# A transformer block on one core: the last 256 columns of the attention gate move from TensorE's rows to GpSimd

## The chip, the cores and the metric

The kernel runs on one core of a Trainium2 chip, written engine by engine: TensorE (PE in the profile) multiplies matrices, VectorE (DVE), ScalarE (ACT) and GpSimd (POOL) work on tiles in SBUF, the on-chip memory of 128 partitions, and SyncE (SP) issues most DMA transfers. TensorE writes to PSUM, which has eight banks. Each engine works through its own list of instructions in order and waits on semaphores where it needs another's result. The metric is the device time of one execution in microseconds (us).

## The reference, cut to what matters

The kernel computes one block of a diffusion transformer: two sequences (batch 2) of 256 tokens, width D = 1152, two attention heads, an MLP of width 4608, all in bfloat16. Six vectors per sequence, computed from a conditioning vector c, shift, scale and gate the two halves of the block.

```python
mod = (_silu(c) @ w_mod).reshape(B, 6, 1, D)
shift_a, scale_a, gate_a, shift_m, scale_m, gate_m = [mod[:, i] for i in range(6)]
h = _layernorm(x, axis=-1) * (1 + scale_a) + shift_a
qkv = (h @ wqkv).reshape(B, N, 3, H, Dh)
...
a = ...softmax(q k^T * Dh ** (-0.5)) v ... @ wo
x = x + gate_a * a
h2 = _layernorm(x, axis=-1) * (1 + scale_m) + shift_m
m = _gelu(h2 @ w_fc1) @ w_fc2
return x + gate_m * m
```

The change is about `gate_a`: 2 x 1152 numbers, each a product of a 1152-vector (the SiLU of c) with a column of `w_mod`.

## The kernel before, in words

All matrices are cut along the contraction into KT = 9 blocks of 128 partitions. The order of TensorE's work is written out by hand: scale and K projection first, then the shift, Q projection, attention scores S with softmax interleaved with the V projection (`v_proj`), the transposes of the softmax tiles (`pt_transposes`), the rest of V, the attention output (`pv`), the output projection (`wo_tile`), the second layer norm, FC1 with GELU and FC2. TensorE and SyncE keep the order in which the program names their work. VectorE, ScalarE and GpSimd get theirs from a planner in the program (`Sched.schedule`): each operation carries an estimated cost, and the planner places an operation when, by these estimates, its inputs are ready, the longest remaining chain first. What it places stays in that order at run time: an instruction whose inputs are late holds up everything behind it on its engine.

The attention gate is made in two ways. Its first FG = 896 columns (NG = 7 groups of 128) are accumulated on VectorE in `attn_gate`. For each block kt and each sequence b, one instruction multiplies the block's weights by a number per partition, L1059 for the first block and L1062 for the others, which also adds the running sum `ACCA`. The 128 partitions are then added up: transposition of 32x32 squares (L1067), a reduction (L1069), three moves and three additions that bring the four groups of 32 partitions together (L1073, L1076), a cast (L1078) and a last transposition (L1079) to a layout in which the gate can be stored to a scratch tensor in DRAM (`st_ga`, from GpSimd's queue).

The last 256 columns come from `rows`, on TensorE: matmuls with two output rows, four of them side by side in the array, 352 columns wide for bank 3 (64 of the gate's, as a quarter of 256, and 288 of the MLP's shift and scale) and 288 wide for bank 4. ScalarE copies the gate's part out (`rows_ev`, L688), and two DMA from GpSimd's queue store it to the scratch tensor (`st_g`). VectorE transposes the rest (L1046).

SyncE's queue then reads the whole gate back, broadcast to all partitions, into `GA` (two transfers, `ld_g`). They stand in its queue behind the first two loads of FC1's weights and ahead of the next two, of the MLP gate's weights and of two quarters of FC2's. In `wo_tile`, VectorE multiplies each 128x384 tile of the output projection by the gate (L1161), which frees one of four PSUM banks for TensorE, GpSimd adds the residual (L1162), and layer norm statistics follow (L741 to L745, L1166), then the normalisation on ScalarE (L1167) and TensorE's transposes of the result (`xn2_T`).

The weights of all these columns lie in one tile, `WMODR`. It is loaded in two sets of three transfers: the columns that VectorE accumulates (`ld_ga`), then, behind the V projection's weights (`ld_wv`), all others (`ld_modr`).

VectorE also does the softmax's maxima (L1001), the normalisation (L1009) and half of the copies out of PSUM (L690). These share its list with the gate's accumulation.

Of the kernel before, what the change touches and what calls it, by code (L numbers as in the profile page):

```python
# [492 lines left out]
F32 = mybir.dt.float32  # L493
ALU = mybir.AluOpType
# [5 lines left out]
D = 1152  # L500
# [8 lines left out]
F0 = 9  # L509
KC = 5  # L510
KG = 6
NG = 7
FG = NG * 128


# [4 lines left out]
def c_act(n, aps=0):  # L520
    return 190.0 + 0.8 * n + 75.0 * aps


def c_dve_psum32(n):
    return 110.0 + 1.13 * n


def c_dve_psum16(n):
    return 110.0 + 0.57 * n
# [14 lines left out]
def build_kernel(nc, x, c, wqkv, wo, w_mod, w_fc1, w_fc2, out):  # L544
    S = Sched()
# [3 lines left out]
    scratch = scratch_t.ap()  # L549
    with (  # L550
# [4 lines left out]
        def sb(off, nbytes, dt=BF16):  # L555
            assert off % 4 == 0 and off + nbytes <= ARENA_BYTES, (off, nbytes)
            v = arena[:, off // 2:(off + nbytes) // 2]
            if dt == F32:
                v = v.bitcast(F32)
            return v  # L560

        def ps32(bank, c0=0, n=512):
            return psum[:, bank * 512 + c0: bank * 512 + c0 + n]
# [7 lines left out]
        W1 = 20736  # L571
        O_A, O_B, O_C, O_R = 0, W1, 2 * W1, 3 * W1
# [7 lines left out]
        O_GA = O_PT + 4096  # L580
        mo = [O_GA + 4608]

        def misc(nbytes):
            o = mo[0]
            mo[0] += (nbytes + 3) // 4 * 4
            assert mo[0] <= ARENA_BYTES
            return o

        def wmat(o, f):
            return sb(o, KT * f * 2).rearrange("p (k f) -> p k f", k=KT)  # L590
# [7 lines left out]
        WMODR = wmat(O_R + W1, 3 * D)  # L598
# [18 lines left out]
        GA = [sb(O_GA + b * 2304, 2304) for b in range(2)]  # L617
        GM = [sb(o + 18432, 2304) for o in (O_A, O_C)]
        XN2 = [sb(O_R + 4 * W1 - (i + 1) * 2304, 2304) for i in range(4)]
        ROWS = sb(O_R + 4 * W1 - 5 * 2304, 2304)[:, 0:288 - 32 * NG]  # L620
        ACCA = sb(O_R, FG * 8, F32).rearrange("p (b d) -> p b d", b=2)
        ACTA = sb(O_R + FG * 8, FG * 8, F32).rearrange("p (b d) -> p b d", b=2)
        GPA = sb(O_R + FG * 16, FG, F32).rearrange("p (q b g) -> p q b g", q=4, b=2)
        GBA = sb(O_R + FG * 17, 128)[0:32, :]
        GTA = sb(O_R + FG * 17 + 128, 128)[0:32, :]
        T1 = [sb(O_X + i * 1536, 1536, F32) for i in range(3)]
        OST = [sb(O_X + 4608 + i * 768, 768) for i in range(3)]
        gt_offs = ([O_P + i * 1024 for i in range(8)] + [O_B + i * 1024 for i in range(20)]
# [11 lines left out]
        ST32 = sb(misc(72), 72, F32)  # L640
# [4 lines left out]
        MT = sb(misc(2304), 2304, F32)  # L645
# [26 lines left out]
        def dma(dst, src, nbytes, name, is_out=False, eng="sp", run=4096):  # L672
            eff = 1.0 if run >= 4096 else (1.08 if run >= 2304 else (1.15 if run >= 1536 else (1.3 if run >= 1024 else 1.42)))
            return S.op(eng, 500.0 if eng == "sp" else 150.0, lambda e: e.dma_start(dst, src), reads=[src], writes=[dst],  # L674
                        name=name, dma_bytes=nbytes * eff, is_out=is_out)

        def dve(cost, fn, reads, writes, name):
            return S.op("dve", cost, fn, reads=reads, writes=writes, name=name)

        def act(cost, fn, reads, writes, name):  # L680
            return S.op("act", cost, fn, reads=reads, writes=writes, name=name)

        def pool(cost, fn, reads, writes, name):
            return S.op("pool", cost, fn, reads=reads, writes=writes, name=name)

        def copy_on(eng, dst, src, n, psum16, name):
            if eng == "act":
                act(c_act(n), lambda e: e.activation(out=dst, in_=src, func=ACTF.Copy), [src], [dst], name)  # L688
            else:
                dve(c_dve_psum16(n) if psum16 else c_dve_psum32(n), lambda e: e.tensor_copy(dst, src), [src], [dst], name)  # L690
# [12 lines left out]
        for (ka, kb, cuts) in ((0, KC, (0, 2, 5, 8, 9)), (KC, KT, (0, 3, 6, 9))):  # L703
            w = (kb - ka) * P
# [10 lines left out]
        def wfc1_load(q):  # L715
# [5 lines left out]
             reads=[ONES], writes=[IDENT], name="ident")  # L721
# [34 lines left out]
        for t in range(4):  # L756
# [13 lines left out]
            for part, c0, c1 in ((("a", 0, KC * P), ("b", KC * P, D)) if t == 3 else (("", 0, D),)):  # L770
                xi, xo = X[:, t, c0:c1], XN[:, t, c0:c1]
                dve(c_dve_fast(c1 - c0), lambda e, xi=xi, xo=xo, m=m, rs=rs: e.tensor_scalar(out=xo, in0=xi, scalar1=m, scalar2=rs,
                                                                                           op0=ALU.subtract, op1=ALU.mult),
# [37 lines left out]
        def quad_mm(bank, w, g0, g1, kt, fresh=True):  # L811
            n = 32 * (g1 - g0)
            for q in range(4):
                o = psum[32 * q:32 * q + 2, bank * 512:bank * 512 + n].rearrange("p (g c) -> p g c", c=32)
                mm(o, ST[:, kt:18:9], quads(w, g0, g1, q), kt == 0 and fresh, kt == KT - 1, tile_position=(0, 32 * q),
                   skip_group_check=not fresh)
# [136 lines left out]
        for kt in range(KT):  # L953
            for b in range(2):
                src, dst = HK[:, kt, b * 256:(b + 1) * 256], HX[:, kt, b * 256:(b + 1) * 256]
# [74 lines left out]
            copy_on("act", V[:, t, ci * CH:(ci + 1) * CH], o, CH, False, "v_ev%d_%d" % (t, ci))  # L1030


        row_parts = ((3, NG, 18), (4, 18, 27))

        last_red = [None]

        def rows():
            S.unit("pe", KT * (864 - 32 * NG) / 2.4 + 500.0, "rows")
            for kt in range(KT):
                for bank, g0, g1 in row_parts:  # L1040
                    quad_mm(bank, WMODR[:, kt, :], g0, g1, kt)
            n = 288 - 32 * NG
            copy_on("act", ROWS, ps32(3, 0, n), n, False, "rows_ev")
            for i, (bank, c0) in enumerate(((3, n), (4, 0))):
                src, dst = ps32(bank, c0, 288), MT[:, i * 288:(i + 1) * 288]
                u = dve(c_dve_psum32(288), lambda e, src=src, dst=dst: e.transpose(dst, src), [src], [dst], "mt_%d" % i)  # L1046
                S.order_after(u, last_red[0])
            sc, so = MT[:, 288:576].rearrange("p (k r) -> p k r", r=32)[:, :, 0:2], SC1M.rearrange("p (k b) -> p k b", b=2)
            dve(170, lambda e: e.tensor_scalar(out=so, in0=sc, scalar1=1.0, scalar2=None, op0=ALU.add), [sc], [so], "sc1m")
            for b in range(2):  # L1050
                dma(scratch[0, b, FG:D].rearrange("(k q c) -> q k c", q=4, c=32), ROWS[b:128:32, :].rearrange("p (k c) -> p k c", c=32),
                    2304 - 2 * FG, "st_g%d" % b, eng="pool")

        def attn_gate():
            for kt in range(KT):
                for b in range(2):
                    o, w, s1 = ACCA[:, b, :], WMODR[:, kt, 0:FG], ST32[:, b * 9 + kt:b * 9 + kt + 1]
                    if kt == 0:
                        dve(150 + FG * 0.6, lambda e, o=o, w=w, s1=s1: e.tensor_scalar(out=o, in0=w, scalar1=s1, scalar2=None, op0=ALU.mult),  # L1059
                            [w, s1], [o], "ga_%d_%d" % (b, kt))  # L1060
                    else:
                        dve(150 + FG * 1.1, lambda e, o=o, w=w, s1=s1: e.scalar_tensor_tensor(out=o, in0=w, scalar=s1, in1=o, op0=ALU.mult, op1=ALU.add),  # L1062
                            [w, s1, o], [o], "ga_%d_%d" % (b, kt))
            pool(100, lambda e: e.memset(GBA, 0.0), [], [GBA], "gba0")
            for b in range(2):
                a_, t_ = ACCA[:, b, :], ACTA[:, b, :]
                dve(150 + FG * 1.1, lambda e, a_=a_, t_=t_: e.transpose(t_, a_), [a_], [t_], "ga_T%d" % b)  # L1067
                t3, o = t_.rearrange("p (g r) -> p g r", r=32), GPA[:, 0, b, :]
                last_red[0] = dve(150 + FG * 1.1, lambda e, t3=t3, o=o: e.tensor_reduce(out=o, in_=t3, axis=AX.X, op=ALU.add), [t3], [o], "ga_red%d" % b)  # L1069
            gp = GPA.rearrange("p q b g -> p q (b g)")  # L1070
            for q in range(1, 4):
                i_, o_ = gp[32 * q:32 * q + 32, 0, :], gp[0:32, q, :]
                dve(200, lambda e, i_=i_, o_=o_: e.tensor_copy(o_, i_), [i_], [o_], "ga_mv%d" % q)  # L1073
            for a_, b_ in ((0, 1), (2, 3), (0, 2)):
                x_, y_ = gp[0:32, a_, :], gp[0:32, b_, :]
                dve(200, lambda e, x_=x_, y_=y_: e.tensor_tensor(out=x_, in0=x_, in1=y_, op=ALU.add), [x_, y_], [x_], "ga_add%d" % b_)  # L1076
            g0, gb = GPA[0:32, 0, :, :], GBA.rearrange("p (b g) -> p b g", b=2)[:, :, 0:4 * NG]
            dve(200, lambda e: e.tensor_copy(gb, g0), [g0], [gb], "ga_bf")  # L1078
            dve(200, lambda e: e.transpose(GTA, GBA), [GBA], [GTA], "ga_t")  # L1079
            for b in range(2):  # L1080
                dma(scratch[0, b, 0:FG].rearrange("(g c) -> g c", c=32), GTA[0:4 * NG, 32 * b:32 * b + 32], FG * 2, "st_ga%d" % b, eng="pool")

        def mlp_gate(prev):
            for b in range(2):
# [59 lines left out]
        def acc_bank():  # L1144
            b = acc[acc_rr[0] % len(acc)]
            acc_rr[0] += 1
            return b
# [76 lines left out]
        pt_transposes(1, 1)  # L1224
        v_proj(2, 0)
        rows()
        wfc1_load(0)
        wfc1_load(1)
# [31 lines left out]
        k = acc_rr[0] % 4  # L1260
# [12 lines left out]
        for t in range(4):  # L1273
            b = t // 2
# [3 lines left out]
            for (c0, c1) in pieces:  # L1278
                w = c1 - c0
                S.unit("pe", JT * c_mm(w), "fc2_%d_%d" % (t, c0))  # L1280
                o = ps32(acc_bank(), 0, w)
# [62 lines left out]
```

## Time and profile before

| | |
|---|---|
| median of 3 runs | 243.71 us (243.59 to 245.18) |
| the profiled execution, its own time | 243.42 us |
| its span in the profile | 241.7 us |
| TensorE busy (PE) | 235.7 us, 98% of the span |
| VectorE (DVE) / ScalarE (ACT) / GpSimd (POOL) busy | 115.9 / 68.0 / 21.4 us |
| granted TensorE clock | 1.00 |

The span runs from the first to the last instruction; the 1.7 us between it and the execution's own time lie around it. A line of the timeline gives the start and the length in us, the engine, the line of the program, the operation, what it writes and reads, shapes and count, and in brackets how long the engine had been idle and what ended that. A line of the groups gives the total busy time, the mean of one in ns, and the idle time before.

### The profile page before, as it was taken

How to read it: one execution, taken by the hardware profiler on the slowest of the kernel's cores; microseconds unless marked ns; L12 is line 12 of the kernel's file. 1: busy time of each engine (PE TensorE's matmuls, PEld its weight loads, DVE VectorE, ACT ScalarE, POOL GpSimd, SP SyncE). 2: the span in 40 equal slices, each digit the busy share in tenths (PEclk: the TensorE clock that was granted, in tenths of full speed). 3: DMA queues.
4: the chain of work that ended last, by engine and by line, in shares of the span. 5: the costliest groups of instructions: out<-in, count | busy, mean ns of one | idle time of the engine just before them, and what ended most of it. 6: DMA issues, size and time to landing. Idle time of an engine off the chain costs nothing.

```text
span 241.7 us, 3956 instructions
## 1 busy us (share of the span) xinstructions
PE 235.7 (98%) x1691; PEld 144.3 (60%) x1699; DVE 115.9 (48%) x229; ACT 68.0 (28%) x137; POOL 21.4 (9%) x38
## 2 busy tenths in 40 slices
PE   6899999999999999999999999999999999999995
PEld 2688844466657666898544444444556666566664
DVE  2654358888994589669999500000122111111112
ACT  4940540546324126973322222333000000000000
POOL 1300000000021476300000110000000000000000
DMA  6999999999994999999963499000000000000000
GB/s 220 369 374 391 390 387 386 404 414 407 391 356 124 321 379 391 392 355 394 343 209 86 122 342 376 8 0 3 0 16 19 16 16 16 19 19 27 22 17 16
DMA packets 30427, 51.58 MB, mean 213 GB/s; under 512 B 1611, under 2 KB 16971, under 8 KB 30411
## 3 DMA queue, kind: packets, MB, share of 16 engines
q1 hardware_dynamic: 29888, 50.73, 58.8%
q0 software_dynamic: 352, 0.60, 0.8%
q8 instruction: 13, 0.21, 0.4%
q10 hardware_dynamic: 171, 0.01, 0.0%
q14 instruction: 3, 0.02, 0.0%
HBM read 50.15 MB, written 1.19 MB: 212 GB/s over the span
## 4 chain that ended last, share of the span: by engine, by line
PE 94%; DMA 3%; SPq 1%; issue 0%; DVE 0%
PE psum L693 92%; DMA arena<-in_wqkv_dram 3%; PE psum L696 2%; SPq L674 1%; DVE arena L1286 0%; DVE arena L1287 0%
## 5 line engine op out<-in xcount | busy, mean ns | idle before, releaser
L693 PE MATMUL psum<-arena 128*128 128x384 bf16 (+9 forms) x1602 | 232.4, 313 | 2.8 <-POOL arena L719 1.5
L693 PEld LDWEIGHTS psum<-arena 128*128 128x128 bf16 (+2 forms) x1610 | 139.0, 97 | 92.0 <-issue 3.8
L1286 DVE TENSOR_TENSOR arena<-psum,arena 128x384 f32<-128x384 f32 (+2 forms) x13 | 6.9, 528 | 88.5 <-PE psum L693 88.5
L1196 ACT ACTIVATE arena<-psum 128x512 bf16<-128x512 f32 (+1 forms) x45 | 22.8, 511 | 42.2 <-PE psum L693 42.2
L688 ACT ACTIVATE arena<-psum 128x512 bf16<-128x512 f32 (+7 forms) x35 | 18.4, 550 | 37.5 <-PE psum L693 37.5
L1091 DVE SCALAR_TENSOR_TENSOR arena<-arena 128x1152 f32<-128x1152 bf16 x16 | 21.3, 1409 | 0.0
L1062 DVE SCALAR_TENSOR_TENSOR arena<-arena 128x896 f32<-128x896 bf16 x16 | 17.7, 1145 | 0.0
L1162 POOL TENSOR_TENSOR arena<-arena 128x384 f32<-128x384 f32 x12 | 10.9, 912 | 13.3 <-DVE arena L1161 11.1
L674 POOL DMA_DIRECT2D dit_scratch<-arena x6 | 3.6, 603 | 92.6 <-ACT arena L688 53.1
L741 DVE BATCH_NORM_STATS2 arena<-arena 128x6 f32<-128x384 f32 (+1 forms) x18 | 9.5, 550 | 4.0 <-DMA arena<-in_x_dram 3.9
L690 DVE CAST arena<-psum 128x512 bf16<-128x512 f32 x11 | 7.5, 690 | 7.4 <-PE psum L693 7.4
L1161 DVE TENSOR_TENSOR arena<-psum,arena 128x384 f32<-128x384 f32 x12 | 6.7, 555 | 3.8 <-PE psum L693 3.8
L1167 ACT ACTIVATE arena<-arena 128x1152 bf16<-128x1152 f32 x4 | 5.4, 1344 | 9.8 <-DVE arena L1166 9.8
L696 PE MATMUL psum<-arena 128*128 128x128 bf16 (+1 forms) x89 | 7.1, 219 | 0.4 <-DMA arena<-in_c_dram 0.4
L696 PEld LDWEIGHTS psum<-arena 128*128 128x128 bf16 (+1 forms) x89 | 5.8, 98 | 2.4 <-DMA arena<-in_c_dram 1.3
L1287 DVE TENSOR_TENSOR arena<-arena 128x384 bf16<-128x384 f32 (+2 forms) x13 | 6.9, 528 | 0.5
L1186 ACT ACTIVATE arena<-psum,arena 128x128 bf16<-128x128 bf16 x16 | 6.1, 455 | 3.0 <-PE psum L696 2.2
L1183 DVE TENSOR_SCALAR arena<-psum,arena 128x128 bf16<-128x128 bf16 x20 | 5.5, 336 | 2.9 <-PE psum L696 2.9
L1005 ACT ACTIVATE arena<-psum,arena 128x256 bf16<-128x256 f32 x8 | 3.7, 469 | 0.4 <-DVE arena L1002 0.3
L745 POOL TENSOR_TENSOR arena<-arena 128x1 f32<-128x1 f32 x6 | 3.3, 553 | 4.5 <-DVE arena L744 4.3
L1001 DVE TENSOR_REDUCE arena<-psum 128x2 f32<-128x512 f32 x4 | 2.7, 686 | 0.9 <-PE psum L693 0.9
L1059 DVE TENSOR_SCALAR arena<-arena 128x896 f32<-128x896 bf16 x2 | 1.3, 684 | 3.6 <-DMA arena<-in_w_mod_dram 3.6
(60 smaller groups left out, 54.1 us busy)
## 6 DMA issues: line engine op xcount, KB each, us to landing
arena<-in_w_fc_dram SPq DMA_DIRECT2D x9, 1152.0 KB, 8.1
arena<-in_w_fc_dram SPq DMA_DIRECT2D x4, 2592.0 KB, 17.5
arena<-in_w_mod_dram SPq DMA_DIRECT2D x3, 1920.0 KB, 19.7
arena<-in_wqkv_dram SPq DMA_DIRECT2D x18, 288.0 KB, 10.0
arena<-in_w_mod_dram SPq DMA_DIRECT2D x3, 864.0 KB, 12.6
arena<-in_wqkv_dram SPq DMA_DIRECT2D x1, 2592.0 KB, 16.9
arena<-in_wo_dram SPq DMA_DIRECT2D x1, 2592.0 KB, 26.1
arena<-in_w_mod_dram SPq DMA_DIRECT2D x1, 2592.0 KB, 18.2
```

Source lines behind the costliest of these rows:

```text
L688: act(c_act(n), lambda e: e.activation(out=dst, in_=src, func=ACTF.Copy), [src], [dst], name)
L690: dve(c_dve_psum16(n) if psum16 else c_dve_psum32(n), lambda e: e.tensor_copy(dst, src), [src], [dst], name)
L693: S.instr(lambda e: e.matmul(o, lhsT=l, rhs=r, start=st, stop=sp, **kw), reads=[l, r], writes=[o])
L696: S.instr(lambda e: e.transpose(o, i_, idn), reads=[i_, idn], writes=[o])
L741: dve(550, lambda e, s=s, o=o: e.bn_stats(out=o, in_=s), [s], [o], "bn_%s_%d" % (tag, ci))
L1062: dve(150 + FG * 1.1, lambda e, o=o, w=w, s1=s1: e.scalar_tensor_tensor(out=o, in0=w, scalar=s1, in1=o, op0=ALU.mult, op1=ALU.add), [w, s1 ...
L1091: u = dve(1300, lambda e, o=o, w=w, s1=s1: e.scalar_tensor_tensor(out=o, in0=w, scalar=s1, in1=o, op0=ALU.mult, op1=ALU.add), [w, s1, o], ...
L1161: dve(550, lambda e, o=o, ga=ga, x1c=x1c: e.tensor_tensor(out=x1c, in0=o, in1=ga, op=ALU.mult), [o, ga], [x1c], "wo_t1_%d_%d" % (t, ci))
L1162: S.op("pool", 930, lambda e, xs=xs, x1c=x1c: e.tensor_tensor(out=x1c, in0=x1c, in1=xs, op=ALU.add), reads=[x1c, xs], writes=[x1c], name=" ...
L1196: act(c_act(ntok), lambda e: e.activation(out=dst, in_=o, func=ACTF.Gelu_apprx_tanh), [o], [dst], "gelu_%d_%d" % (f, tok0))
L1286: dve(c_dve_psum32(w), lambda e, o=o, gm=gm, t1=t1: e.tensor_tensor(out=t1, in0=o, in1=gm, op=ALU.mult), [o, gm], [t1], "fc2_t1_%d_%d" % ( ...
L1287: dve(c_dve_32(w), lambda e, t1=t1, x1c=x1c, ost=ost: e.tensor_tensor(out=ost, in0=t1, in1=x1c, op=ALU.add), [t1, x1c], [ost], "fc2_out_%d ...
```

## The change

NG goes from 7 to 9, so that the accumulated part of the gate is all 1152 columns. `ACCA` keeps one layout; VectorE accumulates its first DG = 896 columns as before, GpSimd the last 256. GpSimd makes a block's contribution in two instructions, a multiplication into a temporary tile (`GTMP`, four buffers in the place of `GA`) and an addition into `ACCA`, since the fused form is VectorE's. VectorE's transpositions and reductions run over 1152 columns instead of 896, for each of the two sequences, and `mt`, the transposition of the rows, no longer waits for ScalarE's copy. The gate's row part, its copy and its two stores go; TensorE's row matmuls for bank 3 shrink from 352 to 288 columns. The store of the gate keeps two transfers in another cut (64 rows of 32 columns, then 8). The loads of `ld_ga` grow by 256 columns per block, those of `ld_modr` shrink by as many.

```diff
-NG = 7
+NG = 9
+DG = 7 * 128
 FG = NG * 128
...
-        row_parts = ((3, NG, 18), (4, 18, 27))
+        row_parts = ((3, 9, 18), (4, 18, 27))
...
-            n = 288 - 32 * NG
-            copy_on("act", ROWS, ps32(3, 0, n), n, False, "rows_ev")
-            for i, (bank, c0) in enumerate(((3, n), (4, 0))):
-                src, dst = ps32(bank, c0, 288), MT[:, i * 288:(i + 1) * 288]
+            for i, bank in enumerate((3, 4)):
+                src, dst = ps32(bank, 0, 288), MT[:, i * 288:(i + 1) * 288]
...
-            for b in range(2):
-                dma(scratch[0, b, FG:D].rearrange("(k q c) -> q k c", q=4, c=32), ROWS[b:128:32, :].rearrange("p (k c) -> p k c", c=32),
-                    2304 - 2 * FG, "st_g%d" % b, eng="pool")
...
                 for b in range(2):
-                    o, w, s1 = ACCA[:, b, :], WMODR[:, kt, 0:FG], ST32[:, b * 9 + kt:b * 9 + kt + 1]
...
+                    for eng, c0, c1, ns in (("dve", 0, DG, 1.1), ("pool", DG, FG, 2.3)):
+                        o, w, s1 = ACCA[:, b, c0:c1], WMODR[:, kt, c0:c1], ST32[:, b * 9 + kt:b * 9 + kt + 1]
+                        if kt == 0:
+                            S.op(eng, 150 + (c1 - c0) * ns, lambda e, o=o, w=w, s1=s1: e.tensor_scalar(out=o, in0=w, scalar1=s1, scalar2=None, op0=ALU.mult),
+                                 reads=[w, s1], writes=[o], name="ga_%s_%d_%d" % (eng, b, kt))
+                        elif eng == "pool":
+                            tmp = GTMP[:, kt % 2 * 2 + b, :]
+                            S.op(eng, 600, lambda e, o=tmp, w=w, s1=s1: e.tensor_scalar(out=o, in0=w, scalar1=s1, scalar2=None, op0=ALU.mult),
+                                 reads=[w, s1], writes=[tmp], name="ga_mul_%d_%d" % (b, kt))
+                            S.op(eng, 600, lambda e, o=o, t=tmp: e.tensor_tensor(out=o, in0=o, in1=t, op=ALU.add),
+                                 reads=[o, tmp], writes=[o], name="ga_acc_%d_%d" % (b, kt))
+                        else:
+                            S.op(eng, 150 + (c1 - c0) * ns, lambda e, o=o, w=w, s1=s1: e.scalar_tensor_tensor(out=o, in0=w, scalar=s1, in1=o, op0=ALU.mult,
+                                                                                                          op1=ALU.add),
+                                 reads=[w, s1, o], writes=[o], name="ga_%s_%d_%d" % (eng, b, kt))
...
-            for b in range(2):
-                dma(scratch[0, b, 0:FG].rearrange("(g c) -> g c", c=32), GTA[0:4 * NG, 32 * b:32 * b + 32], FG * 2, "st_ga%d" % b, eng="pool")
+            lin = scratch[0].rearrange("b (g c) -> (b g) c", c=32)
+            dma(lin[0:64].rearrange("(j p) c -> p j c", j=2), GTA[:, 0:64].rearrange("p (j c) -> p j c", j=2), 4096, "st_ga0", eng="pool")
+            dma(lin[64:72], GTA[0:8, 64:96], 512, "st_ga1", eng="pool")
```

In the changed program the lines shift: L1056 is the first multiplication (on both engines), L1060 and L1062 are GpSimd's further multiplications and its additions, L1065 is VectorE's accumulation step, L1071 and L1073 the transposition and reduction, L1077 to L1083 the moves, additions, cast and last transposition. The planner also places VectorE's work anew: the accumulation steps stand in nearly the same places among the softmax steps, while the three additions, the cast and the last transposition of the gate stand between the copies of the attention output (L691), which stood behind all of them before.

## The prediction, made before the changed kernel was run

> **What bounds the kernel now.** I read the page first (busy shares, chain that ended last), then the timeline of each engine around the gate, then the groups by form.
>
> ```profile
> span 241.7 us, 3956 instructions
> PE 235.7 (98%) x1691; PEld 144.3 (60%) x1699; DVE 115.9 (48%) x229; ACT 68.0 (28%) x137; POOL 21.4 (9%) x38
> PE 94%; DMA 3%; SPq 1%; issue 0%; DVE 0%
> ```
>
> TensorE is busy from 10.9 us to the end, and the chain runs through it: work taken from it is gained one to one, and any wait put into it is lost one to one. So two questions decide: how much shorter is TensorE's own work, and what does TensorE wait for that it found ready before? The second is read from the moments when VectorE's results are due:
>
> ```profile
> 57.86 0.39 PE L696 MATMUL psum<-arena 128*128 128x128 bf16 x4
> 59.54 0.39 PE L696 MATMUL psum<-arena 128*128 128x128 bf16 x4
> 61.23 0.39 PE L696 MATMUL psum<-arena 128*128 128x128 bf16 x4
> 62.91 0.39 PE L696 MATMUL psum<-arena 128*128 128x128 bf16 x4
> ```
>
> These are the transposes of the four softmax tiles. Each needs a normalisation on VectorE (L1009), and the timeline of VectorE shows how full that engine is before them:
>
> ```profile
> 44.91 4.33 DVE L1062 SCALAR_TENSOR_TENSOR arena<-arena 128x896 f32<-128x896 bf16 x4
> 49.15 0.69 DVE L1001 TENSOR_REDUCE arena<-psum 128x2 f32<-128x512 f32 x1
> ...
> 61.61 0.69 DVE L1009 TENSOR_TENSOR arena<-arena 128x512 bf16<-128x512 bf16 x1
> 62.21 2.21 DVE L1062 SCALAR_TENSOR_TENSOR arena<-arena 128x896 f32<-128x896 bf16 x2
> ...
> 72.08 0.23 DVE L1079 STREAM_TRANSPOSE arena<-arena 32x64 bf16<-32x64 bf16 x1
> ...
> 78.05 0.69 DVE L690 CAST arena<-psum 128x512 bf16<-128x512 f32 x1 [0.18 <-PE psum L693]
> ...
> 80.39 0.56 DVE L1161 TENSOR_TENSOR arena<-psum,arena 128x384 f32<-128x384 f32 x1 [0.77 <-PE psum L693]
> ```
>
> The last normalisation ends at 62.30 and is due at 62.91: 0.6 us of slack. From 37 to 70 us VectorE is busy 30.1 of 33 us. The gate leaves VectorE at 72.3 (L1079), is stored, read back from 75.78, and its first half lands 3.5 us later, at 79.3, just ahead of the first use at 80.39 (L1161). The kernel's slack lies in these two places, 0.6 and 1.1 us.
>
> One more reading, from the timeline of both engines, carries the forecast:
>
> ```profile
> 88.34 0.92 POOL L1162 TENSOR_TENSOR arena<-arena 128x384 f32<-128x384 f32 x1
> 88.64 0.63 DVE L1166 SCALAR_TENSOR_TENSOR arena<-arena 128x1 f32<-128x1 f32 x1
> 92.72 0.92 POOL L1162 TENSOR_TENSOR arena<-arena 128x384 f32<-128x384 f32 x1
> 93.11 0.55 DVE L1166 SCALAR_TENSOR_TENSOR arena<-arena 128x1 f32<-128x1 f32 x1
> 99.57 0.16 DVE L1166 SCALAR_TENSOR_TENSOR arena<-arena 128x1 f32<-128x1 f32 x1
> ```
>
> The same one-column instruction takes 0.16 us alone, but 0.63 and 0.55 when GpSimd is adding: it ends at 89.27 and 93.66, the GpSimd adds at 89.26 and 93.64. An instruction of VectorE with two SBUF operands is held until the running GpSimd instruction is done. BN_STATS (one SBUF operand) keeps 0.55 under the same adds. The gate's L1062 is that two-operand instruction, 16 times, and the normalisation L1009 too.
>
> **The change, part by part.** Rows on TensorE: 36 matmuls of 352 columns become 288. Four run side by side (72 matmuls of these rows take 2.5 us), and nine of 384 columns take 1.46 us, 2.36 columns per ns; 9 x 64 / 2.36 = 0.24 us less. That is all TensorE gains. ScalarE's L688 copy of the rows (0.22) and two stores on POOL's queue (1.39) go, none of them on the path.
>
> Loads: the three gate loads ahead of WV grow from 672 to 864 KB. They landed 1.9 us apart, so each takes 0.55 longer; the gate starts at 37.9 instead of 37.3, and WV lands at 49.4 instead of 47.8, due at 51.7: hidden, with 2.3 us left. The row loads behind shrink by as much.
>
> GpSimd: 18 multiplications and 16 additions of 128x256. The trace has neither shape.
>
> ```profile
> L1162 POOL TENSOR_TENSOR arena<-arena 128x384 f32<-128x384 f32 x12 | 10.9, 912 | 13.3 <-DVE arena L1161 11.1 <-DVE arena L744 2.1
> L1062 DVE SCALAR_TENSOR_TENSOR arena<-arena 128x896 f32<-128x896 bf16 x16 | 17.7, 1145 | 0.0
> ```
>
> Addition: 0.912 us for 384 columns with some 0.17 fixed (the 18-column cast of L735 takes 0.19) gives 0.66; bounds 0.50 and 0.67. Multiplication, one tensor read: from that cast (0.19) and the 128-column select of L719 (0.28), 0.0008 us a column, 0.39; bounds 0.30 and the addition's 0.67. I take 0.66 and 0.39, the nearest rows: 16 x 0.66 + 18 x 0.39 = 17.6 us, mean 0.52 (0.40 to 0.67).
>
> The hold: each two-operand instruction of VectorE should find a GpSimd instruction running, and the next GpSimd instruction then waits for it in turn (L754 took 0.83 instead of 0.57 when issued under a VectorE L772). I price one mean GpSimd instruction, 0.52, per L1062, L1009 and also the two L1059 that open the gate. Along the new VectorE order: gate from 37.9; 2 x (0.60 + 0.52) + 3 x (1.07 + 0.52) = 44.9; two copies, 46.2; four L1062, 52.6; first maximum 53.2 (before: 49.8). Then maxima (0.61), five more L1062 and four normalisations (0.60 + 0.52) alternate; these end at 58.4, 61.9, 64.2 and 68.6. Queued behind each held instruction are the softmax steps, and TensorE's transposes wait for them: 58.5 against 57.86 (0.6), then, each time shifted by the stalls so far, 1.8, 0.6 and 2.8: **5.8 us**. Bounds with 18 held instructions: 18 x 0.12 less, 3.6; 18 x 0.15 more, 8.5.
>
> The sum over the gate: three L1062 to 73.4, transposition 1.42 (1.105 x 1152/896), the second softmax copy 0.4, the last L1062 1.6, reduction 1.36, the second transposition to 79.5 (GpSimd's last add, some 77.5, is ahead of it), the two row transpositions 0.75, reduction 1.36, moves and first add 0.9: 82.5. The wider transpositions and reductions, 1.2 us, lie in here. In the new order the remaining gate steps stand between the copies of the attention output (L691, each 0.69, before L690), which came behind the whole gate before. Three copies, two adds, a cast and the last transposition (L1083, before L1079): 86.0. Two things follow. The third copy is late for the bank that the last attention product takes: 0.7 us on TensorE. And the gate is stored from 86.3; the store of this shape, later in the trace (4 KB), lands 2.3 us after issue, the two of 1.8 KB 3.1 and 2.7; then 3.5 for the read: the gate is there at 92.2 to 93.0, its first product done by 92.8 to 93.6. TensorE, 6.5 us late by then, starts the output projection at 85.2 and fills its four banks by 91.1: **1.7 to 2.5 us** more.
>
> Behind that: GpSimd must do six residual adds of 0.91 before the first rstd; four are due at once. Counted from the first product's end, adds to 5.5, rstd 6.1, two BN_STATS, a product and L1171 to 6.9 or, held, 7.5, normalisation on ScalarE 1.35: 8.3 to 8.9. TensorE is at its transposes after five tiles of 1.46, 7.3: **1.0 to 1.6**; before, this had 1.2 us of slack.
>
> SP's queue stands behind the gate's read-back: it goes on at some 89.3 instead of 75.8, and with it two FC1 loads, the MLP gate's weights and two quarters of FC2. The fifth FC1 load, behind all of them, comes at some 134 instead of 119.5; TensorE needs it at some 130, plus the 10 us it is late itself. Hidden with about 6 us left. The MLP gate starts with VectorE's queue, not its load, and is needed 60 us later.
>
> Sum: 5.8 + 0.7 + 2.1 + 1.3 - 0.24 = 9.7. Against the profiled execution, 243.4 (span 241.7 and 1.7 around it), 253.1; that one ran 0.3 under the median of 243.7, so **253.4 us**. With the bounds, 250 to 257.
>
> **The rivals.** (1) No hold at this size: the two L1166 waited for something that only their one column shows. Then GpSimd is done by 57 and the softmax is on time. The gate is still late by the new order: L1083 follows the copy that ended at 78.74, so 78.75; plus 0.3, 2.3 to 3.1, 3.6: 85.0 to 85.7, product done 85.5 to 86.3; TensorE is out of banks at 84.3. It loses 1.2 to 1.9 and 1.0 behind it, less 0.24: some 245.6, about half of its outcomes within 1%. It decides if L1062 keeps 1.15 under GpSimd's adds. Against it: two ends that agree within 0.02 us.
> (2) GpSimd keeps its hold from one instruction to the next. VectorE then starts at 37.9 + 17.6 = 55.5, the copies of 43.7 come at 61.2, where TensorE needs them at 47.7: 13.5 us, and 1.9 for the gate's order: 258.9. Against it: L754 waited for VectorE.
> (3) TensorE slows after its waits. Its first seven matmuls of 512 columns start 0.42 us apart, later ones 0.22. Two stretches of some 3.4 us at half speed, after the last softmax wait and the gate's, add 3.4: 256.8. No row shows a slowdown later on; the granted clock is 1.00 throughout. The Trainium skill, "TensorE: Matmul & The Clock Gate", Part 1, states that about 3.4 us of idle halves the clock; by that rule none of my single waits is quite long enough, and the trace has no wait to test it.
> (4) That TensorE gains without a loss needs the gate stored by 80 us, against an order that puts its last step behind three copies.
>
> On (2), the Trainium skill, "SBUF — State Buffer", section "Who interferes with whom", says that whoever issues first has the shared ports for the whole instruction and the other blocks; it names no turn-taking. The rows of L1166 agree on the blocking.
>
> **How the numbers follow.** Forecast 0.62; (1) 0.13; (2) 0.12; (3) 0.10; faster or equal by (4) 0.03. A change of about 1%, 2.4 us, is what a measurement can tell. Half of (1) and part of (4) are within it, 0.07; faster 0.02; slower 0.91. The range takes the forecast's own 250 to 257, (3), (2) with 1.6 above, and the upper edge of (1): 246.5 to 260.5.
>
> **What would show it** (line numbers of the changed kernel). L1065, the gate's step, near 1.6 us mean instead of 1.15, its ends on GpSimd's; TensorE waiting before the four transposes (some 6 us in all) and again on the gate's products (L1166 there) in the output projection; L1083 near 86; SP's read-back near 89. Wrong if L1065 stays near 1.15, if GpSimd's instructions are under 0.3 us, or if TensorE has no idle time between 57 and 66.

## The result, and the profile after

The changed kernel takes 251.1 us (median of 6 runs, 249.3 to 252.5) against 243.5: 1.030 times as long, 95% interval 1.026 to 1.034. The forecast, 253.4 us, had the direction, and its range held the time, but most of the loss came by another way than forecast. Of the experiments' executions, one of e6 (248.1 us) and one of e8 (1414.9 us, for no known reason, and the one that was profiled) lie far above the others and are left out of the ratios below. The profiled execution took 249.31 us, the fastest of the six; its page begins:

```profile
span 247.8 us, 3994 instructions
## 1 busy us (share of the span) xinstructions
PE 238.2 (96%) x1699; PEld 144.6 (58%) x1699; DVE 119.8 (48%) x229; ACT 68.0 (27%) x136; POOL 58.4 (24%) x70
```

GpSimd is busy 37 us longer, VectorE 3.9. What TensorE waited for, longest first (us in total, times, longest); only these three are new:

```profile
PE psum L694 <- DVE arena L691: 3.2, 1, 3.2
...
PE psum L697 <- DVE arena L1010: 0.4, 1, 0.4
...
PE psum L694 <- DVE arena L1045: 0.2, 1, 0.2
```

The timeline of TensorE says where. Compare the transposes' starts with 57.86, 59.54, 61.23 and 62.91 before:

```profile
58.30 0.39 PE L697 MATMUL psum<-arena 128*128 128x128 bf16 x4
59.99 0.39 PE L697 MATMUL psum<-arena 128*128 128x128 bf16 x4
61.68 0.39 PE L697 MATMUL psum<-arena 128*128 128x128 bf16 x4
63.96 0.40 PE L697 MATMUL psum<-arena 128*128 128x128 bf16 x4 [0.43 <-DVE arena L1010]
...
78.17 1.48 PE L694 MATMUL psum<-arena 128*128 128x256 bf16 x12 [0.21 <-DVE arena L1045]
82.83 15.45 PE L694 MATMUL psum<-arena 128*128 128x256 bf16 x85 [3.18 <-DVE arena L691]
98.12 0.67 PE L697 MATMUL psum<-arena 128*128 128x128 bf16 x9
```

TensorE enters this part 0.4 us late, which it already was at its first K projection (11.33 instead of 10.91), before anything of the gate has run; this differs from profile to profile (57.8 to 58.9 for the first transpose in the experiments). The softmax costs 0.6 (5.66 us from the first to the last of the four transposes, instead of 5.05). Then one long wait: the last attention product needs a PSUM bank that VectorE's third copy has not emptied. And then TensorE is slow without waiting. The windows (length, busy time of each engine, granted clock PEclk, DMA) show it:

```profile
core 0: us, PE busy (x) PEld busy (x) DVE busy (x) ACT busy (x) POOL busy (x), PEclk, DMA share, GB/s
...
78.00:83.00 5.00, 1.65 (x14) 1.24 (x15) 4.87 (x15) 1.19 (x2) 0.00 (x0) 1.00 0.00 0
83.00:90.00 7.00, 7.00 (x36) 3.88 (x34) 1.88 (x5) 0.60 (x1) 1.32 (x2) 0.76 0.40 82
```

Before the change TensorE had no gap there and a clock of 1.00:

```profile
78.00:84.00 6.00, 6.00 (x42) 3.85 (x40) 3.65 (x7) 1.19 (x2) 1.87 (x3) 1.00 1.01 307
```

The trace's clock records hold a granted clock of 0.5 from 83.9 to 87.3 us; matmuls of 384 columns start 0.32 us apart there, and 0.16 from 87.4 on. The sum against before, by TensorE's starts: 0.4 at the start, 0.6 softmax, 0.24 less for the rows (2.31 instead of 2.55 us), 3.75 from the first attention product to the output projection (7.81 instead of 4.06), 1.7 for the half clock, 0.1 less behind it: 6.1, the difference of the spans, 247.8 and 241.7.

### The profile page after: what moved, and what is told of

It is laid out like the page before. It is cut to its first block, busy times and chain, and to the rows that moved or that the text cites. A ratio compares the mean times of both kernels' runs of the same rounds, so it can differ in the third digit from the quotient of the medians.

```text
span 247.8 us, 3994 instructions
## 1 busy us (share of the span) xinstructions
PE 238.2 (96%) x1699; PEld 144.6 (58%) x1699; DVE 119.8 (48%) x229; ACT 68.0 (27%) x136; POOL 58.4 (24%) x70
## 4 chain that ended last, share of the span: by engine, by line
PE 71%; POOL 15%; DMA 8%; DVE 3%; SPq 1%; issue 0%; DVEq 0%
PE psum L694 70%; POOL arena L1060 9%; POOL arena L1062 6%; DMA arena<-in_w_mod_dram 5%; DMA arena<-in_wqkv_dram 3%; PE psum L697 1%; SPq L675 1%; POOL arena L1056 1%; DVE arena L691 1%; DVE arena L1071 1%; DVE arena L1073 0%; DVE arena L1045 0%; DVE arena L1077 0%; DVE arena L1080 0%; DVE arena L1291 0%
## 5 line engine op out<-in xcount | busy, mean ns | idle before, releaser
L694 PE MATMUL psum<-arena 128*128 128x384 bf16 (+8 forms) x1610 | 234.8, 314 | 6.1 <-DVE arena L691 3.2
L689 ACT ACTIVATE arena<-psum 128x512 bf16<-128x512 f32 (+6 forms) x34 | 18.2, 560 | 40.1 <-PE psum L694 39.6
L1060 POOL TENSOR_SCALAR arena<-arena 128x256 f32<-128x256 bf16 x16 | 21.8, 1368 | 0.0
L1065 DVE SCALAR_TENSOR_TENSOR arena<-arena 128x896 f32<-128x896 bf16 x16 | 21.1, 1355 | 0.0
L1062 POOL TENSOR_TENSOR arena<-arena 128x256 f32<-128x256 f32 x16 | 14.5, 906 | 0.2
L675 POOL DMA_DIRECT2D dit_scratch<-arena x4 | 2.5, 618 | 44.0 <-DVE arena L1111 36.3
L691 DVE CAST arena<-psum 128x512 bf16<-128x512 f32 x11 | 7.4, 678 | 4.0 <-PE psum L694 4.0
L1056 POOL TENSOR_SCALAR arena<-arena 128x256 f32<-128x256 bf16 x2 | 2.6, 1298 | 22.4 <-DMA arena<-in_w_mod_dram 22.4
L1071 DVE STREAM_TRANSPOSE arena<-arena 128x1152 f32<-128x1152 f32 x2 | 2.8, 1378 | 4.2 <-POOL arena L1062 4.2
```

The source lines that it names most:

```text
L694: S.instr(lambda e: e.matmul(o, lhsT=l, rhs=r, start=st, stop=sp, **kw), reads=[l, r], writes=[o])
L1060: S.op(eng, 600, lambda e, o=tmp, w=w, s1=s1: e.tensor_scalar(out=o, in0=w, scalar1=s1, scalar2=None, op0=ALU.mult), reads=[w, s1], writes ...
L1062: S.op(eng, 600, lambda e, o=o, t=tmp: e.tensor_tensor(out=o, in0=o, in1=t, op=ALU.add), reads=[o, tmp], writes=[o], name="ga_acc_%d_%d" % ...
L1065: S.op(eng, 150 + (c1 - c0) * ns, lambda e, o=o, w=w, s1=s1: e.scalar_tensor_tensor(out=o, in0=w, scalar=s1, in1=o, op0=ALU.mult, op1=ALU. ...
```

## What VectorE and GpSimd do to each other

The groups (busy us, mean ns of one, idle before it) show both engines busy; VectorE's step was 1145 ns before:

```profile
L1060 POOL TENSOR_SCALAR arena<-arena 128x256 f32<-128x256 bf16 x16 | 21.8, 1368 | 0.0
...
L1065 DVE SCALAR_TENSOR_TENSOR arena<-arena 128x896 f32<-128x896 bf16 x16 | 21.1, 1355 | 0.0
L1062 POOL TENSOR_TENSOR arena<-arena 128x256 f32<-128x256 f32 x16 | 14.5, 906 | 0.2
```

How they slow each other is read from single rows of the timeline:

```profile
53.66 1.75 POOL L1060 TENSOR_SCALAR arena<-arena 128x256 f32<-128x256 bf16 x1
54.89 0.68 DVE L1010 TENSOR_TENSOR arena<-arena 128x512 bf16<-128x512 bf16 x1
...
59.66 0.88 POOL L1062 TENSOR_TENSOR arena<-arena 128x256 f32<-128x256 f32 x1
59.87 1.62 DVE L1065 SCALAR_TENSOR_TENSOR arena<-arena 128x896 f32<-128x896 bf16 x1
60.52 1.76 POOL L1060 TENSOR_SCALAR arena<-arena 128x256 f32<-128x256 bf16 x1
61.49 1.28 DVE L1065 SCALAR_TENSOR_TENSOR arena<-arena 128x896 f32<-128x896 bf16 x1
62.25 1.10 POOL L1062 TENSOR_TENSOR arena<-arena 128x256 f32<-128x256 f32 x1
62.69 1.21 DVE L1010 TENSOR_TENSOR arena<-arena 128x512 bf16<-128x512 bf16 x1
```

The step lasts 1.14 us undisturbed. If it keeps this length once it has begun, the one that starts at 59.87 under an addition and ends at 61.49 began its own 1.14 at 60.35, 0.19 before the addition's end (60.54). The one at 61.49 under a multiplication ends at 62.77: it began at 61.63, 0.65 before the multiplication's end (62.28). So VectorE is held during a part of GpSimd's instruction, not for all of it. The normalisation at 54.89 agrees: it keeps its 0.68 us although the multiplication around it runs on to 55.41. The one at 62.69 was held under an addition, 1.21 us instead of 0.69, and the last transposes waited for it. Behind an addition the step loses at most 0.47 us (a step of 1.61), behind a multiplication 0.22 (1.36), 0.21 in the mean of 16. GpSimd pays more: a multiplication takes 0.91 us alone, and up to 1.90, most often 1.76, when it is issued under such a step (1.37 in the mean of all 16); an addition takes 0.72 and 1.10. GpSimd works from 37.8 to 76.3 with 0.2 us of idle time, and both of VectorE's transpositions wait for it; 4.2 us of idle time before the two transpositions are GpSimd's:

```profile
76.36 1.38 DVE L1071 STREAM_TRANSPOSE arena<-arena 128x1152 f32<-128x1152 f32 x1 [1.94 <-POOL arena L1062]
...
83.41 0.26 DVE L1083 STREAM_TRANSPOSE arena<-arena 32x96 bf16<-32x96 bf16 x1
```

Behind this come reductions, moves and copies in VectorE's list; the third copy ends at 82.78, and TensorE goes on at 82.83.

## The experiments

My theory after reading the profile (A): the loss is GpSimd's late end, made by its own length and by the shared access to SBUF together. Rivals: (B) the new order and the wider sums on VectorE; (C) GpSimd alone is as slow; for the slow stretch, that the clock falls for a reason other than the wait.

**e1, the change again**

> The changed kernel once more, as the base for the three runs beside it. Its profile showed TensorE waiting 0.6 us in the softmax and 3.7 us in the attention output (0.4 for the row transpositions, 3.3 for VectorE's copies out of PSUM), then 3.4 us at a granted clock of 0.5, and GpSimd busy from 37.8 to 76.3 us. Every theory expects the same here: 249 to 252.5 us, the waits in the same places.

250.7 us, 1.029 (1.022 to 1.036). The waits are in the same places: 0.4, 0.2 and 3.2 us. The clock stays at 0.5 for 6.83 us this time, twice 3.41, from 82.1 on. Its first 1.1 us lie in the wait, which ends at 83.2, and 5.7 us behind it: 2.9 us lost instead of 1.7. One source of the spread between runs of this kernel is therefore how long the clock stays down behind the same wait. It is not the only one: of the ten executions in the result and here, those whose mean granted clock (0.993) fits one stretch of 3.41 took 249.0 to 251.2 us, those that fit two (0.986) 250.8 to 252.5, and one at 1.00 all through took 251.4.

**e2, without GpSimd's work**

```diff
                         elif eng == "pool":
+                            continue
```

> GpSimd's 32 multiplications and additions for blocks 1 to 8 are left out (the gate's last 256 columns hold block 0 alone); the order of every engine is held to that of the changed kernel. Theory A, that the loss comes from GpSimd's chain (its own length, stretched by the shared SBUF access): the step L1065 goes back to 1.15 us, the first transposition no longer waits, the last copy that TensorE waited for is back on TensorE's own time, and what is left is the order: the gate's last transposition near 79, the gate in SBUF near 84.5, at most 1 us of waiting in the output projection; 243.3 to 244.8 us. Rival B, that the new order on VectorE (gate steps between the copies) and the wider sums are the loss by themselves: the wait before the last attention product stays over 2 us and the time at 247 or more.

244.4 us, 1.0034 (1.0021 to 1.0047). VectorE's step takes 1156 ns, no wait before the attention product, 0.5 us for the first product with the gate and 0.4 behind it. (B) is refuted as the main cause: order and wider sums are worth 0.8 us together.

**e3, without VectorE's steps**

```diff
-                        else:
+                        elif eng == "pool":
```

The branch below this line is VectorE's step. The branch ahead of it already takes GpSimd's work, so nothing comes to it any more.

> The other side alone: VectorE's 16 steps L1065 for blocks 1 to 8 are left out (its 896 columns hold block 0 alone), GpSimd's work and all orders stay. Theory A with the shared access as the stretch: GpSimd's 18 multiplications take 0.91 and its 16 additions 0.72 us each, as in the few stretches of the changed kernel where VectorE ran no such step, 27.9 us in all, so it ends at 65.7 instead of 76.3; no wait in the softmax; 243.2 to 244.5 us. Rival C, that GpSimd is as slow by itself and VectorE has no part in it: GpSimd still ends at 74 or later, and the wait before the last attention product stays near 3 us, 248 us or more.

244.2 us, 1.0026 (1.0014 to 1.0038). The groups:

```profile
L1060 POOL TENSOR_SCALAR arena<-arena 128x256 f32<-128x256 bf16 x16 | 15.1, 945 | 0.0
L1062 POOL TENSOR_TENSOR arena<-arena 128x256 f32<-128x256 f32 x16 | 11.9, 749 | 0.2
```

GpSimd ends at 67.7, 2 us later than expected but 8.6 before its end in the change, and its instructions take nearly what they take alone. (C) falls. With either engine's part alone the kernel is 0.8 (e2) or 0.6 us (e3) over before, with both about 7: the loss is their meeting. As e3 also frees VectorE of its 16 steps, the time alone would not show this; e6 keeps both engines full.

**e4, the wait filled**

```diff
             for g in range(g0, g0 + 4):
+                if (b, g) == (1, 7):
+                    for i in range(14):
+                        mm(ps32(2), IDENT, Q4B, True, True)
```

> Fourteen matmuls of 512 columns that nothing reads (into a free PSUM bank, 14 x 0.215 = 3.0 us) are put before the last attention product's second half, where TensorE waited 3.3 us; all orders as in the changed kernel. Theory: the wait itself costs the clock. Then TensorE runs at a granted clock of 1.00 through the output projection, starts it at the same time, and wins 1.7 us there; but its four banks are then full near 89.1 us while the gate lands near 89.3, so it waits 0.5 to 0.9 us on the first product: 248.2 to 248.6 us where the base takes 249.3. Rival: the clock drops for another reason (a fixed moment, power): no change, or 3 us slower where the matmuls come on top.

251.8 us, 1.033 (1.029 to 1.036); the expected time is missed. Half of the theory held: the granted clock is 1.00 from 83 to 90 us and in all four executions of this kernel, against one of ten without the added matmuls. The wait need not be the only cause of a fall: two executions of the kernel before, at 245.3 and 245.4 us, have a mean of 0.993 too, and no profile shows why. But TensorE's waits are now

```profile
PE psum L694 <- DVE arena L1169: 1.9, 1, 1.9
PE psum L694 <- DVE arena L1045: 1.7, 1, 1.7
```

GpSimd ended at 77.7 here, 1.4 us later than in the change's profile, before any of the added matmuls ran; so the row transpositions came late, and then the gate's product. What the clock no longer cost, the later gate did. Why GpSimd ended later in this profile is open.

**e5, VectorE accumulates everything**

```diff
-DG = 7 * 128
+DG = 9 * 128
...
-                    for eng, c0, c1, ns in (("dve", 0, DG, 1.1), ("pool", DG, FG, 2.3)):
+                    for eng, c0, c1, ns in (("dve", 0, DG, 1.1),):
```

> VectorE accumulates all 1152 columns, GpSimd none; one layout and one store as in the change, rows of 288 on TensorE, the planner's own order. No instruction of GpSimd reads SBUF beside the 16 steps, so they should take 1.41 us (the row of the same size in the MLP gate) instead of 1.15, 4.3 us more in all. The planner puts five steps behind the last normalisation, so the softmax is on time, and the sum over the gate comes late by about 6 us against the kernel before: the gate's last transposition near 82, one wait of 1 to 1.5 us before the last attention product and 2 to 3 us for the first product with the gate; 247.5 us (245.5 to 248.5). Theory A (GpSimd and VectorE slow each other) expects this to be faster than the changed kernel, though VectorE does more; a theory by which GpSimd takes work off a full VectorE expects it slower, 251 or more.

250.1 us, 1.027 (1.025 to 1.029): 2.6 over what was expected, and about the changed kernel's time. The step takes 1407 ns and the softmax is on time (0.2 us), as expected, but the first product with the gate is waited for 4.6 us, not 2 to 3, and the clock drops for 3.4 us behind it. VectorE idled 1.9 us ahead of the two Q copies in its list, and the gate's last transposition came at 82.8, behind all five copies. TensorE was also 1.0 us late by 16 us already, before any step of the gate. Theory A expected e5 to be faster than the change; 1.027 and 1.029 cannot be told apart. So giving 256 columns to GpSimd bought nothing: it spares VectorE 16 x (1.41 - 1.14) = 4.3 us, and costs it 16 x 0.21 = 3.4 us of longer steps and 4.2 us of waiting for the last additions.

**e6, GpSimd writes and does not read**

```diff
-                            S.op(eng, 600, ... e.tensor_scalar(...) ...)
-                            S.op(eng, 600, ... e.tensor_tensor(...) ...)
+                            for what in ("mul", "acc"):
+                                S.op(eng, 600, lambda e: e.memset(GTMP, 0.0), writes=[GTMP], name="ga_%s_%d_%d" % (what, b, kt))
```

> GpSimd's 32 instructions are replaced by 32 memsets of 128x1024 that write and read nothing (some 0.9 us each by the small memsets, so GpSimd is as busy as alone, near 30 us; the gate's last 256 columns hold block 0 alone); all orders as in the changed kernel. If VectorE is held by GpSimd's reads, the step L1065 takes 1.15 us while GpSimd is just as busy, and the time is that of the run without GpSimd's work, 244.4 us (243.9 to 245.0). If any GpSimd instruction holds it, the step stays near 1.35 us, the memsets are stretched as the additions were, and the time is 248 or more.

244.4 us, 1.0031 (1.0020 to 1.0042). The groups:

```profile
L1061 POOL MEMSET arena<- 128x1024 f32 x32 | 30.4, 951 | 1.7
```

```profile
L1063 DVE SCALAR_TENSOR_TENSOR arena<-arena 128x896 f32<-128x896 bf16 x16 | 17.7, 1142 | 0.0
```

GpSimd is as busy as in e3, and VectorE's step is undisturbed. It is GpSimd's reads that hold VectorE. The memsets feed nothing, so e6 also takes away VectorE's wait for the last addition: it shows the hold, and not how the loss divides between the longer steps and that wait. The Trainium skill, "SBUF — State Buffer", section "Who interferes with whom", states just this: a VectorE instruction with two SBUF inputs contends with a GpSimd instruction that reads SBUF, not with one that only writes; e6 agrees. The same section calls the shared ports an exclusive lock and, of the modes that use two ports, says that the other engine blocks for the whole instruction; for this pair the rows above differ (0.22 us lost behind a multiplication that takes 0.91 alone), and they decide here.

**e7, without GpSimd's work, gate ahead of the copies**

> As the run without GpSimd's 32 instructions (same part left out), but on VectorE the gate's remaining steps stand ahead of the five copies of the attention output, as in the kernel before. That run was 0.8 us over before, with 0.5 us of waiting for the first product with the gate and 0.4 behind it. If the order among the copies is the cause of these, the gate leaves VectorE near 73.5 to 74.5 instead of 79, both waits go and the time is 243.1 to 243.6 us. If the wider loads, transpositions and stores cost the 0.8, it stays at 244.2 or more.

In VectorE's list the moves, additions, cast and last transposition stand ahead of the five copies. 242.9 us, 0.9974 (0.9964 to 0.9985). The last transposition is at 74.7 and both waits are gone: the 0.8 us of e2 were the order among the copies. The time is 0.2 us under what was expected and 0.7 under before, with GpSimd's work left out; 0.24 of it are TensorE's rows, the rest was not traced.

**e8 and e10, the whole change, copies ahead of the gate**

> The whole change with GpSimd's work, but on VectorE the two row transpositions and all five copies of the attention output stand ahead of the gate's second transposition, which waits for GpSimd's last addition. If GpSimd's late end is the loss and the order only chooses where it shows, the wait before the last attention product (3.2 us) goes and comes back at the first product with the gate: copies done near 80, the gate's last transposition near 84.5, the gate in SBUF near 90, TensorE out of banks near 85.5, 4.5 to 5.5 us of waiting, and a clock of 0.5 for one or two stretches of 3.4 us behind it; 250.5 to 253 us. If the order is the loss, the time falls to 247 or less.

> The same kernel as in e8, for a profile: no wait before the last attention product, one of 4.5 to 5.5 us at the first product with the gate, and a clock of 0.5 for one or two stretches of 3.4 us behind it, if GpSimd's late end is the loss and the order chooses only where it shows.

The two row transpositions and five copies go ahead of the gate's second transposition by hand. 251.7 us, 1.033 (1.032 to 1.035), in e10, one execution, 251.8. In e10's profile the wait before the attention product is gone, and

```profile
PE psum L694 <- DVE arena L1165: 5.7, 1, 5.7
```

```profile
86.00:95.00 9.00, 3.55 (x12) 1.71 (x13) 3.42 (x7) 0.00 (x0) 4.37 (x6) 0.63 0.66 163
```

The wait stands at the first product with the gate, 5.7 us, a little over what was expected, and the clock is at 0.5 for 6.83 us from 88.4 on, in the wait and behind it. GpSimd ended at 76.5 as before. With GpSimd late, the order only chooses the place.

**e9, VectorE alone, relieved**

Besides the edit of e5 and an order of the engines given by hand:

```diff
-            copy_on("dve" if b == 0 else "act", PTS[idx].rearrange("p j k -> p (j k)"), ps16(bank, 0, 512), 512, True, "PT_ev%d" % idx)
+            copy_on("act", PTS[idx].rearrange("p j k -> p (j k)"), ps16(bank, 0, 512), 512, True, "PT_ev%d" % idx)
...
-            copy_on("dve", OT[:, 4, :], ps32(5), 512, False, "OT_ev_4")
+            copy_on("act", OT[:, 4, :], ps32(5), 512, False, "OT_ev_4")
```

> VectorE accumulates all 1152 columns as in e5, but loses three copies out of PSUM to ScalarE (two softmax tiles, one of the attention output, 1.5 us), runs four steps instead of two before the Q copies, where e5 idled 1.9 us, and finishes the gate ahead of its remaining four copies. If e5 was slow because VectorE's list was full, the last step ends 2.5 us earlier by TensorE's clock, the gate's last transposition near 76.5 instead of 82, the gate lands before 84 and no wait is left: 243.0 us (242.8 to 244.0), with the 0.24 us of the narrower rows as the gain. If wide steps cost something else (the wider loads, the store's cut), it stays at 245 or more.

243.4 us, 0.9989 (0.9970 to 1.0007): not to be told from before, 0.4 over what was expected. The last transposition is at 78.0, 1.5 later than expected, yet TensorE waits nowhere but 0.2 us in the softmax. With the same layout, loads and store as the change, all of e5's loss is gone (250.1 to 243.4 us) by what VectorE does and when. Three things changed at once, the copies given to ScalarE, the order of the steps and the gate ahead of the copies, and no run separates them, or gives the changed kernel itself this relief. A gain of 0.24 us is smaller than this interval.

## Why the prediction was right or wrong

- **The number**: that 253.4 lies near 251.1 is in good part luck. Of the 5.8 + 0.7 + 2.1 + 1.3 us forecast as waits, the profile shows 0.6, 3.4, 0 and 0; 1.7 us come from the half clock, a rival in the prediction, and 0.4 from a start that was late before anything of the gate had run.
- **TensorE's rows**: 0.24 us predicted, 0.24 measured.
- **Loads and SP's queue**: right. The gate's loads landed at 37.7 to 43.2 and WV at 49.9, ahead of its use. SP went on behind the gate at 85.9 (89 predicted) and no later transfer was waited for.
- **GpSimd's instructions**: the term was mis-sized. Additions 0.66 predicted, 0.72 measured; multiplications 0.39, with 0.67 as the upper bound, and 0.91 measured. My nearest rows, a cast of 18 columns and a select of 128, had no number per partition and no bfloat16 tile of this width. 17.6 us were predicted for the chain; 29.6 in e3.
- **The hold**: that GpSimd holds VectorE was right, and e6 shows it with its condition. How long was wrong: 0.52 us for each step predicted, 0.21 measured. I took it that VectorE is held until GpSimd's instruction ends, because two ends agreed within 0.02 us. But these two had 0.16 us of own work, so they began some 0.15 before the additions' ends, much as the step above began 0.19 before one; the agreement was chance. The softmax wait was 0.6 instead of 5.8 us. Of the other side, GpSimd held by VectorE, I had seen one row (L754) and taken it as turn-taking, with no price on GpSimd's chain; it made the multiplications half as long again in the mean (1.37 against 0.91 us).
- **The gate's end**: near by luck, as GpSimd's instructions were priced too short and the hold on VectorE too long: GpSimd's last addition at 77.5 predicted, 76.3 measured, L1083 at 86.0 and 83.4.
- **Copies in VectorE's list**: 0.7 us predicted for the third copy, 3.2 measured. Since the softmax cost 5 us less than forecast, TensorE came to that bank 5 us earlier, while the copy came only 2.6 earlier with the gate's steps: 0.7 + 5.2 - 2.6 = 3.3. The 2.1 us for the first product with the gate and the 1.3 behind it did not come: the gate was there in time, because TensorE had already waited and then ran at half clock.
- **Rivals**: (1), no hold, and (2), GpSimd keeping it, are refuted by the rows above. (3), the slower clock, came true, 1.7 us in the profile and 2.9 in e1. I held it back because none of my single waits was long enough; the waits in or behind which it fell were 3.2 to 5.7 us long, and waits up to 1.9 us (e4) had none. The Trainium skill's page "TensorE: Matmul & The Clock Gate" has about 3.4 us of idle time in Part 1; 3.2 of wait were enough here. In the four profiles with a fall, TensorE had worked 0.8 to 1.4 of the last 3.41 us before it, and in e4 at least 1.5 of any 3.41 us around its waits; no run tests where the limit lies. (4) fell with the gate's store, issued at 84.0 and not by 80.

## What to carry to other kernels

Work given to GpSimd is not free for VectorE: where both read SBUF, price it on both engines, and count what the slower chain's end holds up, not its busy time. When a number rests on an agreement of ends, check it with a second duration: here the 1.14 us step showed that the hold ends before the other instruction does. And when one predicted stall turns out small, look at once for the place where the same lateness is due next.

## What the runs showed of the hardware that I had not expected

GpSimd's multiplication of 256 bfloat16 columns by a number per partition, to float32, takes 0.91 us, longer than its addition of two float32 tiles of that width (0.72). With the same wait of 3.2 us on TensorE the granted clock was 0.5 for 3.41 us in one run, where it fell 1.1 us behind the wait's end, and for 6.83 in another, where it fell 1.1 us ahead of it.
